# A fused attention and MoE kernel: another order of loads, units and banks at the start, weights loaded in pieces, another split of the last tile, longer half-chunks in two chunks

## The chip, the cores and the metric

The kernel runs on one core of one Trainium2 chip. The metric is device time in microseconds (us). Kernels are compared only within the same rounds. All timed runs that are compared are "fast" (none more than 1.5% above the fastest of its kernel).

## The reference, cut to what matters

```python
def _attn_ref(q, k, v):                       # (8 batches, 8 heads, 576 tokens, 64)
    scores = scale * q @ k.T                  # per batch and head
    mask = (rel >= 0) & (rel < 128)           # a sliding window of 128 tokens
    scores = where(mask, scores + slope[h] * -abs(rel), -1e9)
    return softmax(scores) @ v

def _moe_ref(x, w_in, w_out):                 # x: 4608 x 512, w_in: 512 x 2048
    h = x @ w_in                              # "MoE1"
    g = h * cos(h)
    return g @ w_out                          # "MoE2"
```

The attention's output is laid out as 4608 tokens of 512 columns and goes through the two matrix products. Inputs and output are float32; inside, the matmuls work on bf16.

## The kernel before

A small planner in the program (class `Plan`) takes the operations with guessed durations, dependencies and priorities, and fixes one order of instructions for every engine. The order cannot change at run time, and each engine runs its own in order. Where the planner expects PE to wait in the head, it puts in "fillers", matmuls of zeros.

The tokens go through MoE in 9 chunks of 512, the attention in 8 batches of 576. A chunk is MoE1 (matmul, then cosine on ScalarE and a product on VectorE) and MoE2 (matmul, copy, store). While chunk c is in MoE2, the attention of batch c+1 is woven in. A batch has 9 "units": four pairs of heads for tokens 0 to 255 ("first token group"), four for tokens 256 to 511, and a tail. ScalarE needs one table for exp (attention) and one for the cosine (MoE1); the page counts 15 table loads of 1.28 us each. An attention unit is scores, exp, mask, product with v, division, and turning the result (`xnat`) so that MoE1 can read it (`xT`):

```python
def x_back(b, u, s, i):
    ...
    pr, G = u                                   # G: token group
    t0 = S * b + 256 * G
    if b >= 3 or (b == 2 and G):                # later batches: by a transposing DMA
        o = op("sp", [lambda e: e.dma_start_transpose(
            xT[:, pr, t0:t0 + 256].rearrange("p (r t) -> p r t", r=2), xnat[i][:, :])], ...)
        xops.append(o)
        return
    ...                                         # early ones: TensorE turns, a copy follows
```

MoE1 of a chunk begins with "half" jobs, which read only 256 of its 512 tokens, so that it can start while the rest of `xT` is on its way. With SPLIT = 4 the first 8 of 16 column blocks are done in halves, first all of the first half, then all of the second, and the other 8 whole:

```python
n = (0, 8, SPLIT, SPLIT, SPLIT, SPLIT, SPLIT, SPLIT, 0)[c]
for i in range(2 * n):
    moe1_half(c, i // n, i % n, 2 + i % 6)
for i in range(16 - 2 * n):
    moe1(c, 2 * n + i, 2 + (2 * n + i) % 6)
```

Loads go through GpSimd (POOL) and convert float32 to bf16 on the way. The first ones are the head of the program; a batch's loads wait for the transposing DMAs of an earlier batch:

```python
load_first("q", q, 0, 0, "sp")      # heads 0-3, first token group
load_first("k", k, 0, 1, "sp")
...
load_half("q", q, 1)                # heads 4-7, first token group
load_half("k", k, 1)
load_v(0, (0, 1))
masks()
load_piece("q", q, 0, 1)            # second token group, 256 KB in bf16
load_piece("k", k, 0, 1)
load_w_in(0)                        # 512 of 2048 columns
load_v(0, (2, 3))
load_w_in(1)
load_w_in(2)
...                                 # tails, w_in, w_out and batch 1 mixed
# in the loop over chunks c:
if c == 0:
    load_batch(2)
elif c + 3 < B:
    load_batch(c + 3, xops[-1:])    # so batch 4 waits for batch 2's tail to land in xT
```

The last of the 36 tiles of the output is computed with 512 columns, then copied and stored in two halves:

```python
halves = 2 if tg == 4 * NCH - 1 else 1
wd = 512 // halves
for hf in range(halves):
    cs = slice(wd * hf, wd * hf + wd)
    flex(ob[oi][:, cs], ps[:, bank, cs], ...)                 # copy on ScalarE or VectorE
    op("sp", [lambda e, cs=cs: e.dma_start(out[row:row + 128, cs], ob[oi][:, cs])], ...)
```

The softmax here doesn't subtract the row's maximum and nothing guards it: scores larger than these inputs give would overflow.

## Time and profile before

| | before |
|---|---|
| time, median of 3 first runs (range) | 316.63 us (316.44 to 316.78) |
| profiled run: time, span | 317.92 us, 315.9 us |
| TensorE (PE) busy | 307.1 us, 97% |
| useful matmuls at the price of their shape | about 286 us |
| before the first matmul / after the last | 1.2 us / 3.2 us |

The profiled run was itself 1.3 us over the median.

From the profile's page of the kernel before: the span, busy time by engine, the busy tenths of PE and DMA in 40 slices of the span, and the chain that ended last by engine and by line (L843 is MoE2, L832 MoE1 in halves, L817 MoE1 whole, L611 scores).

```profile
span 315.9 us, 6775 instructions
...
PE 307.1 (97%) x2702; PEld 180.1 (57%) x2702; DVE 195.9 (62%) x440; ACT 208.2 (66%) x307; POOL 100.6 (32%) x127
...
PE   7989999999998999999999999999999999999995
...
DMA  9999999999979995599969999997813200101121
...
PE 88%; DMA 5%; ACT 3%; DVE 3%; issue 1%; POOL 0%; POOLq 0%; ACTq 0%
PE ps L843 37%; PE ps L832 20%; PE ps L817 17%; PE ps L611 5%; DMA xT<-xnat 4%; ACT p L648 2%; PE ps L705 2%; PE ps L708 1%; PE ps L526 1%; DMA qnat<-in_q_dram 1%; DVE xnat L747 1%; PE ps L780 1%; PE ps L396 1%; PE ps L691 1%; PE ps L601 1%
```

PE carries 88% of the chain, and DMA is the only other entry over 3%. PE's busy time hides stalls, because a matmul's record is longer than the distance to the next one. So I priced each matmul with the spacing of starts in a dense stretch (216 ns for 512 columns, 109 ns for 256, 29 ns for 65, 56 ns for 128) and call what exceeds that price a stall. The DMA row shows that the DMA engines are full through the first 11 slices, about 87 us.

The head, in the timeline of ScalarE (start, us, engine, line, operation, output and input, count, and in brackets the idle time before it with what ended it). The first two lines are the four exps of the first token group, the third the four of the second one, then the change to the cosine's table, then the first cosines.

```profile
7.73 1.51 ACT L648 ACTIVATE p<-ps 128x768 bf16<-128x768 f32 x2 [0.16 <-PE ps L611]
10.44 1.51 ACT L648 ACTIVATE p<-ps 128x768 bf16<-128x768 f32 x2 [1.20 <-PE ps L611]
...
15.86 3.77 ACT L648 ACTIVATE p<-ps 128x1024 bf16<-128x1024 f32 x4 [0.23 <-PE ps L611]
19.65 1.28 ACT L471 ACT_TABLE_LOAD   x1
...
21.05 1.25 ACT L803 ACTIVATE cos<-ps,halfpi 128x512 f32<-128x512 f32 x2
```

Two waits for `xT` on PE. In the first pair of lines it waits before chunk 2's second half; in the second pair, within chunk 3's first half (timeline of PE, kernel before).

```profile
92.55 1.91 PE L832 MATMUL ps<-xT,w_inb 128*128 128x256 bf16 x16
95.58 0.72 PE L832 MATMUL ps<-xT,w_inb 128*128 128x256 bf16 x5 [1.13 <-DMA xT<-xnat]
...
121.21 0.38 PE L832 MATMUL ps<-xT,w_inb 128*128 128x256 bf16 x2
121.95 0.28 PE L832 MATMUL ps<-xT,w_inb 128*128 128x256 bf16 x1 [0.36 <-DMA xT<-xnat]
```

The bracket counts from the modelled end of the last matmul, so 1.13 is 1.3 us in spacing of starts, and 0.36 is 0.5. The sum of both stands in the view of waits (who waited for whom: us in total, times, longest):

```profile
PE ps L832 <- DMA xT<-xnat: 1.5, 2, 1.1
```

The chain of the kernel before, as a list in order of time, gives the DMA that the second wait was for: from issue to landing it took over 7 us.

```profile
114.56 7.35 DMA xT<-xnat
```

The end (timeline of all engines, kernel before): the last matmuls, the stores' issues, and two copies of 256 columns that ScalarE makes one behind the other.

```profile
307.79 4.91 PE L843 MATMUL ps<-w_outb,gT 128*128 128x512 bf16 x22
...
310.02 4.05 SPq L858 DMA_DIRECT2D out_dram<-ob  x3
312.80 0.80 ACT L401 ACTIVATE ob<-ps 128x256 f32<-128x256 f32 x2 [2.86 <-PE ps L843]
```

### The profile page before, as it was taken

The page shows a single profiled execution, that of the slowest core. Times are in us where ns is not written, and L with a number is a line of the kernel's source. Part 1 is how long each engine was busy: PE and PEld are TensorE (multiplying, and loading weights), DVE is VectorE, ACT ScalarE, POOL GpSimd, SP SyncE. Part 2 cuts the span into 40 slices and gives each one's busy share as a digit, 9 for nine tenths or more (in the row PEclk, how much of TensorE's full clock was granted, in tenths as well). Part 3 has the DMA queues.
Part 4 walks back from the last instruction along what each step waited for, and adds up shares of the span by engine and source line. Part 5 has one row for each costly group of instructions (what it writes and reads, how often), then busy time and mean ns, then how long its engine had stood idle before and what let it go on. Part 6 is the DMA issues. An engine that isn't in the chain of part 4 may idle for free.

```text
span 315.9 us, 6775 instructions
## 1 busy us (share of the span) xinstructions
PE 307.1 (97%) x2702; PEld 180.1 (57%) x2702; DVE 195.9 (62%) x440; ACT 208.2 (66%) x307; POOL 100.6 (32%) x127
## 2 busy tenths in 40 slices
PE   7989999999998999999999999999999999999995
PEld 4468645685565456645764575458545844444442
DVE  3887576687666766767687578658865880353000
ACT  7788776788586857783887488739866883462211
POOL 8997650008706900491029206900000000000000
PEclk9999999999999999999999999999999999999999
DMA  9999999999979995599969999997813200101121
GB/s 124 175 197 200 192 165 193 165 138 80 183 98 111 156 174 138 93 137 172 152 99 154 191 122 133 172 183 96 150 50 87 50 0 35 67 0 68 66 97 69
DMA packets 157582, 38.97 MB, mean 123 GB/s; under 512 B 147696, under 2 KB 153072, under 8 KB 157552
## 3 DMA queue, kind: packets, MB, share of 16 engines
q0 software_dynamic: 107392, 18.10, 75.6%
q1 hardware_dynamic: 50160, 20.46, 34.1%
q8 instruction: 21, 0.34, 0.5%
q14 instruction: 9, 0.07, 0.1%
HBM read 36.70 MB, written 9.44 MB: 146 GB/s over the span
## 4 chain that ended last, share of the span: by engine, by line
PE 88%; DMA 5%; ACT 3%; DVE 3%; issue 1%; POOL 0%; POOLq 0%; ACTq 0%
PE ps L843 37%; PE ps L832 20%; PE ps L817 17%; PE ps L611 5%; DMA xT<-xnat 4%; ACT p L648 2%; PE ps L705 2%; PE ps L708 1%; PE ps L526 1%; DMA qnat<-in_q_dram 1%; DVE xnat L747 1%; PE ps L780 1%; PE ps L396 1%; PE ps L691 1%; PE ps L601 1%
## 5 line engine op out<-in xcount | busy, mean ns | idle before, releaser
L843 PE MATMUL ps<-w_outb,gT 128*128 128x512 bf16 x576 | 139.4, 379 | 0.0
L809 DVE TENSOR_TENSOR gT<-ps,cos 128x512 bf16<-128x512 f32 x144 | 94.7, 685 | 33.5 <-ACT cos L803 16.6
L803 ACT ACTIVATE cos<-ps,halfpi 128x512 f32<-128x512 f32 x144 | 94.7, 686 | 25.3 <-PE ps L832 8.3
L843 PEld LDWEIGHTS ps<-w_outb,gT 128*128 128x128 bf16 x576 | 51.5, 98 | 51.9 <-issue 0.9
L832 PE MATMUL ps<-xT,w_inb 128*128 128x256 bf16 x640 | 77.0, 273 | 2.3 <-DMA xT<-xnat 1.5
L648 ACT ACTIVATE p<-ps 128x768 bf16<-128x768 f32 (+1 forms) x64 | 54.5, 917 | 24.9 <-PE ps L611 13.0
L832 PEld LDWEIGHTS ps<-xT,w_inb 128*128 128x128 bf16 x640 | 59.9, 98 | 13.1 <-DMA xT<-xnat 2.0
L435 POOL DMA_DIRECT2D qnat<-in_q_dram x32 | 28.4, 888 | 96.5 <-DMA xT<-xtail 69.7
L817 PE MATMUL ps<-xT,w_inb 128*128 128x512 bf16 x256 | 56.7, 379 | 0.0
L401 ACT ACTIVATE ob<-ps 128x512 f32<-128x512 f32 (+1 forms) x24 | 13.9, 581 | 44.5 <-PE ps L843 44.4
L817 PEld LDWEIGHTS ps<-xT,w_inb 128*128 128x128 bf16 x256 | 25.0, 98 | 28.8 <-DVE gT L809 0.5
L444 POOL DMA_DIRECT2D vp<-in_v_dram x40 | 34.9, 939 | 5.7 <-issue 5.6
L666 DVE TENSOR_TENSOR p<-p,emask 128x1024 bf16<-128x1024 bf16 x32 | 22.0, 687 | 18.8 <-ACT p L648 18.8
L435 POOL DMA_DIRECT2D knat<-in_k_dram x32 | 28.6, 894 | 0.6 <-issue 0.6
L747 DVE TENSOR_TENSOR xnat<-ps,rec 128x256 bf16<-128x256 f32 x64 | 26.8, 421 | 2.0
L705 PEld LDWEIGHTS ps<-vp,p 128*128 128x128 bf16 x256 | 17.1, 97 | 14.4 <-issue 9.4
L705 PE MATMUL ps<-vp,p 128*128 128x65 bf16 x256 | 22.0, 193 | 0.4 <-DVE p L673 0.3
L708 PE MATMUL ps<-vp,p 128*128 128x65 bf16 x192 | 20.0, 193 | 0.0
L671 DVE TENSOR_TENSOR p<-p,emask 128x256 bf16<-128x256 bf16 x32 | 9.0, 282 | 17.4 <-ACT p L648 17.1
L471 ACT ACT_TABLE_LOAD x15 | 19.2, 1283 | 0.3
L611 PEld LDWEIGHTS ps<-qt,kt 64*128 64x128 bf16 x320 | 12.3, 95 | 11.6 <-issue 8.0
L611 PE MATMUL ps<-qt,kt 64*128 64x128 bf16 (+1 forms) x320 | 17.6, 244 | 0.5 <-DVE xT L402 0.4
(58 smaller groups left out, 169.5 us busy)
## 6 DMA issues: line engine op xcount, KB each, us to landing
out_dram<-ob SPq DMA_DIRECT2D x35, 256.0 KB, 4.1
vp<-in_v_dram POOLq DMA_DIRECT2D x32, 128.0 KB, 10.3
qnat<-in_q_dram POOLq DMA_DIRECT2D x25, 128.0 KB, 7.6
knat<-in_k_dram POOLq DMA_DIRECT2D x25, 128.0 KB, 7.9
w_inb<-in_moe_w_in_dram POOLq DMA_DIRECT2D x4, 512.0 KB, 10.8
w_outb<-in_moe_w_out_dram POOLq DMA_DIRECT2D x4, 512.0 KB, 18.0
qnat<-in_q_dram POOLq DMA_DIRECT2D x3, 256.0 KB, 17.1
knat<-in_k_dram POOLq DMA_DIRECT2D x3, 256.0 KB, 17.6
```

Of the source, the lines that this page charges most:

```text
L435: op("pool", [lambda e: e.dma_start(nat[w][b % 2][0:rows, t, :].rearrange("p (h d) -> p h d", h=H), src[b, :, 128 * t:128 * t + rows, :].r ...
L444: op("pool", [lambda e, t=t, rows=rows: e.dma_start(vp[b % 2][0:rows, t, :, 0:64], v[b, :, 128 * t:128 * t + rows, :].rearrange("h p d -> ...
L611: ins = e.matmul(ps[:, banks[x], c0:c1], keys_ap(i, x, pr, kc), query_ap(i, x, pr, qb, nb), start=True, stop=True)
L648: op("act", lambda e: e.activation(P[i][:, :, lo:512], src_[:, :, lo:512], ACTF.Exp, scale=0.125), w=held + [("P", i)], occ=920 if u[1] el ...
L705: ins = e.matmul(o, P[i][:, x, d0:d0 + 128], V[:, kc, h, 0:65], start=True, stop=not two)
L708: ins = e.matmul(o, P[i][:, x, p0:p0 + 128], V[:, kc - 1, h, 0:65], start=False, stop=True)
L747: op("dve", lambda e: e.tensor_tensor(o, U[:, :, :, 0:64], rv[:, :, :, None].broadcast_to([128, 2, 2, 64]), ALU.mult), r=[("rec", ri)], w= ...
L803: op("act", lambda e: e.activation(cosb[ci][:, :], h, ACTF.Sin, bias=halfpi[:, 0:1]), r=["halfpi"], w=[("B", bank), ("cos", ci)], occ=586, ...
L809: op("dve", lambda e: e.tensor_tensor(o, h, cs, ALU.mult), r=[("cos", ci)], w=[("B", bank)] + keys, occ=606, lat=692, pri=3)
L817: op("pe", lambda e, kc=kc: e.matmul(ps[:, bank, :], w_in[:, kc, 128 * fc:128 * fc + 128], xT[:, kc, CH * c:CH * c + CH], start=(kc == 0), ...
L832: op("pe", lambda e, i=i, fc=fc, kc=kc: e.matmul(ps[:, bank, 256 * i:256 * i + 256], w_in[:, kc, 128 * fc:128 * fc + 128], xT[:, kc, t0:t0 ...
L843: op("pe", lambda e, fc=fc: e.matmul(ps[:, bank, :], gT[gi][:, fc, 128 * t:128 * t + 128], w_out[:, fc, :], start=(fc == 0), stop=(fc == N ...
```

## The change

Its intent is to bring the start of the program closer together, so that PE is dense earlier: another order of the first loads (the later queries first, v before the weights), w_in mostly in pieces of 256 columns, another order of units and PSUM banks in batches 0 and 1. Besides, chunks 2 and 3 get 6 pairs of halves instead of 4, and the last tile is split into 384 and 128 columns, so that only a short copy and a short store follow the last matmul. The small buffers of reciprocals are separated for units and tails.

```diff
+FIRST = [("k", "q", 0, 1), ("h", "k"), ("h", "q"), ("v", 0, 0), ("v", 0, 1), ("k", "k", 0, 1),
+         ("v", 0, 2), ("v", 0, 3), ("i", 6, 2), ("i", 2, 2), ("i", 4, 2), ("i", 0, 2),
+         ("i", 12, 2), ("i", 8, 4), ("m",), ("i", 14, 2), ("k", "q", 1, 0), ("v", 0, 4),
+         ("t", "k", 0), ("o", 0, 4), ("k", "k", 1, 0), ("t", "q", 0), ("o", 4, 4), ("o", 8, 4),
+         ("v", 1, 0), ("v", 1, 1), ("o", 12, 2), ("o", 14, 2), ...]
+HEAD = [("T", "k", 0, 0, 3), ("T", "q", 0, 2, 3), ("R", (3,), (1,)), ("T", "q", 1, 7, 6), ...]
+JOBS = [(0, 6, 6), (0, 1, 1), (0, 2, 3), (1, 4, 1), (0, 4, 2), (0, 3, 5), ...]
+SECOND = [("T", "k", 0, 2, 2), ("F", 0, 6), ("T", "q", 0, 3, 3), ("R", (2,), (3,)), ...]
 ... cut: the reciprocals' buffers; keys of single 128-column blocks of w_in and w_out
-        def load_w_in(u):
+        def load_w_in(u, n=4):
 ... cut: loads n blocks of 128 columns; the same for w_out
 ... cut: the list of loads is read from FIRST, the units of batch 0 and 1 from HEAD and SECOND,
 ... the half jobs of chunk 0 from JOBS
-            halves = 2 if tg == 4 * NCH - 1 else 1
 ... cut
+                cols = [(0, 512, OB[t % 2])] if c < NCH - 1 or t < 3 else [(0, 384, 1), (384, 128, 2)]
+                for c0, wd, bank in cols:
+                    moe2_mm(c, t, bank, c0, wd)
+                    store(c, t, bank, c0, wd)
-                n = (0, 8, SPLIT, SPLIT, SPLIT, SPLIT, SPLIT, SPLIT, 0)[c]
+                n = (0, 8, 6, 6, SPLIT, SPLIT, SPLIT, SPLIT, 0)[c]
```

In FIRST, "k" is a 256 KB piece of q or k, "h" a half load of heads 4 to 7, "v" a block of v, "i" and "o" blocks of w_in and w_out, "t" a tail, "m" the masks.

## The prediction

> **What bounds the kernel.** TensorE. The page shows PE busy 307.1 of 315.9 us, clock full. Busy hides stalls, so I took the spacing of matmul starts in the timeline: a 512-column matmul costs 216 ns, a 256-column one 109 ns, a 65-column one with its own weight load 29 ns. This agrees with the Trainium skill, "TensorE: Matmul & The Clock Gate", "Back-to-back issue gap". At these prices the useful matmuls take about 286 us; the other 30 us are: 1.2 us before the first matmul, about 12.8 us of filler and stalls in 0 to 25 us, about 7 us in 25 to 100, about 5.5 us later, 3.2 us after the last matmul.
>
> **What the change does, step by step.**
>
> 1. Head (0 to 35 us). Same work, but queries of tokens 256 to 511 load first, v blocks 0 to 3 before the weights, w_in mostly in 256-column pieces. Issues on POOL: 34 instead of 32 at about 0.9 us. In the timeline the exps of the second token group start at 15.9 us, because their keys land at 12.85; the Sin table arrives at 20.9; MoE1 is dense only from 22 to 24 us. With the queries transposed while engines idle (DVE idles 3.2 us before 8.3), I expect these exps 1 to 1.5 us earlier, Sin at about 19.5, MoE1 dense from 19 to 20.5. w_in arrives at about the old rate (512 columns per 2.6 us between landings), so its first piece lands no earlier, about 15.5. Gain 2.5 us, between 1 and 4.
> 2. Batch 1 (35 to 65 us). Stalls sum to about 4 us, perhaps 2 avoidable (0.67 at 60.9, 0.42 at 40.2). But the DMA list shows landings back to back from 10 to 47 us (w_out complete at 41.1, last batch-1 v at 47.4); a PE that comes earlier meets w_out and batch 1 nearly when it did. Gain 0.7 us.
> 3. Longer halves. Before chunk 2's second half PE stands 1.3 us at 94.2 (in the waits: MoE1 halves for the DMA-transposed x). Four more half jobs are 16 more 256-column matmuls, 1.74 us of work ahead of that need: the wait disappears. The wait at 121.3 (0.5 us, chunk 3) is for the *first* half, so longer halves do not help, and PE, earlier now, may wait there more: those transposes took 7 to 9 us to land while batch 4 loaded.  Net gain 0.9 us.
> 4. Last tile. 16x512 columns (3.45 us) become 16x384 and 16x128 (2.6 + 0.9 us, estimate from the fitted spacing): equal. After the last matmul two copies of 0.39 us ran one behind the other on ACT; now one of 128 columns and a smaller store. Gain 0.5 us.
>
> Sum: 4.6 us, all on TensorE's path.
>
> **Predicted: 312.0 us, range 309.0 to 315.0.** Faster by over 2% (below 310.3): 0.25; within 2%: 0.73; slower: 0.02.
>
> **What would show it.** Step 1: Sin table load at 18 to 19.5 us (now 19.65), stalls in 0 to 25 us about 10.5 (12.8). Step 2: stalls in 35 to 65 at about 3 us. Step 3: no stall over 0.3 us near 90; the one near 118 equal or longer. Step 4: last matmul to end 2.7 us (3.2). Matmul work itself unchanged at about 286 us.
>
> **What would make it wrong.** Better: MoE1 begins at 15 us and the whole program moves up 4 us. Worse: loads of batches 0 to 3 set the pace; then PE's lead of the head comes back as waits for transposed x at chunks 2 and 3, and only the tail's half microsecond stays.

## The result, and the profile after

The kernel after took 314.97 us (median of 4, 314.78 to 315.88) against 316.53 us (316.12 to 316.78). A ratio here is the mean time of one kernel's fast runs over the mean of the other's of the same rounds, so it is not quite the ratio of the medians. It was 0.9958 (95% interval 0.9935 to 0.9980). Two later repeats on other chips gave 0.9909 and 0.9917. The mean of the three ratios, 0.993, is 2.3 us: half of the 4.6 us that I had forecast, and the first measurement is a third of it.

From the page of the kernel after (all line numbers are 16 to 18 higher: L861 is MoE2, L850 MoE1 in halves, L835 MoE1 whole, L629 scores):

```profile
span 312.9 us, 6840 instructions
...
PE 300.8 (96%) x2712; PEld 183.6 (59%) x2748; DVE 196.3 (63%) x441; ACT 207.0 (66%) x306; POOL 103.7 (33%) x131
...
PE   7699999999999998999999999999999999999996
...
DMA  9999999999999995999599999995713100201112
...
PE 84%; DMA 6%; POOL 4%; ACT 2%; issue 1%; DVE 1%; POOLq 0%; ACTq 0%
PE ps L861 37%; PE ps L850 21%; PE ps L835 15%; PE ps L629 4%; DMA w_inb<-in_moe_w_in_dram 4%; PE ps L723 2%; DMA xT<-xnat 2%; PE ps L726 2%; ACT cos L821 1%; POOL w_inb L468 1%; POOL vp L461 1%; DVE gT L827 1%; PE ps L709 1%; PE ps L711 1%; PE ps L798 1%
```

PE's busy time has fallen by 6 us, but that is no measure of gain: some matmul records are missing in this trace (the page counts 564 matmuls of MoE2 beside 592 of its weight loads). DMA's share of the chain has not fallen: 4% of it is now a load of w_in, which PE waits for in the head.

ScalarE in the head of the kernel after:

```profile
6.54 1.51 ACT L666 ACTIVATE p<-ps 128x768 bf16<-128x768 f32 x2 [0.43 <-PE ps L629]
...
10.65 0.81 ACT L666 ACTIVATE p<-ps 128x768 bf16<-128x768 f32 x1 [0.43 <-PE ps L629]
12.54 0.81 ACT L666 ACTIVATE p<-ps 128x768 bf16<-128x768 f32 x1 [1.08 <-PE ps L629]
...
15.01 3.77 ACT L666 ACTIVATE p<-ps 128x1024 bf16<-128x1024 f32 x4
18.64 0.42 ACT L417 ACTIVATE xT<-ps 128x256 bf16<-128x256 bf16 x1
19.06 1.28 ACT L489 ACT_TABLE_LOAD   x1
...
20.73 1.26 ACT L821 ACTIVATE cos<-ps,halfpi 128x512 f32<-128x512 f32 x2
```

The first two exps start 1.2 us earlier than before, but the third and fourth, which ran as a pair at 10.44, now start at 10.65 and 12.54. Those of the second token group start 0.85 us earlier, the table 0.6 us, the first cosine 0.3 us. In before the table load follows the last exp at once; here the planner has put a copy of `xT` (18.64) between them, which will matter below. PE's waits in the first 35 us (kernel after) show loads among their causes:

```profile
PE ps L723 <- issue: 1.1, 1, 1.1
PE ps L544 <- ACT kt L417: 0.8, 1, 0.8
PE ps L850 <- DMA w_inb<-in_moe_w_in_dram: 0.7, 1, 0.7
PE ps L544 <- DMA qnat<-in_q_dram: 0.6, 1, 0.6
```

A wait named "issue" was for nothing that this view shows. The one of 1.1 us at L723 ends at 11.7 us, just as the second block of v lands (11.61 in the trace's records of DMAs).

PE at chunk 2's second half and at chunk 3's first half (timeline, kernel after):

```profile
91.23 5.95 PE L850 MATMUL ps<-xT,w_inb 128*128 128x256 bf16 x53
...
118.19 0.38 PE L850 MATMUL ps<-xT,w_inb 128*128 128x256 bf16 x2
119.40 0.28 PE L850 MATMUL ps<-xT,w_inb 128*128 128x256 bf16 x1 [0.83 <-DMA xT<-xnat]
```

The wait of 1.13 us in chunk 2 is gone: 53 half matmuls run through. The wait in chunk 3 grew from 0.36 to 0.83 us. The chain of the kernel after names the same kind of DMA, again 7 us long:

```profile
112.20 7.15 DMA xT<-xnat
```

And the end (kernel after):

```profile
304.83 5.60 PE L861 MATMUL ps<-w_outb,gT 128*128 128x512 bf16 x41
...
307.70 3.40 SPq L875 DMA_DIRECT2D out_dram<-ob  x3
309.63 0.49 ACT L417 ACTIVATE ob<-ps 128x384 f32<-128x384 f32 x1 [2.00 <-PE ps L861]
310.46 0.28 ACT L417 ACTIVATE ob<-ps 128x128 f32<-128x128 f32 x1 [0.34 <-PE ps L861]
```

One copy of 0.28 us follows the last matmul, instead of two of 0.8 us in sum.

### The profile page after: what moved, and what is told of

The parts are those of the page before. It is cut to its first block, busy times and chain, and to the rows that moved or that the text cites. A ratio compares the mean times of both kernels' runs of the same rounds, so it can differ in the third digit from the quotient of the medians.

```text
span 312.9 us, 6840 instructions
## 1 busy us (share of the span) xinstructions
PE 300.8 (96%) x2712; PEld 183.6 (59%) x2748; DVE 196.3 (63%) x441; ACT 207.0 (66%) x306; POOL 103.7 (33%) x131
## 4 chain that ended last, share of the span: by engine, by line
PE 84%; DMA 6%; POOL 4%; ACT 2%; issue 1%; DVE 1%; POOLq 0%; ACTq 0%
PE ps L861 37%; PE ps L850 21%; PE ps L835 15%; PE ps L629 4%; DMA w_inb<-in_moe_w_in_dram 4%; PE ps L723 2%; DMA xT<-xnat 2%; PE ps L726 2%; ACT cos L821 1%; POOL w_inb L468 1%; POOL vp L461 1%; DVE gT L827 1%; PE ps L709 1%; PE ps L711 1%; PE ps L798 1%
## 5 line engine op out<-in xcount | busy, mean ns | idle before, releaser
L861 PE MATMUL ps<-w_outb,gT 128*128 128x512 bf16 (+2 forms) x564 | 132.4, 373 | 2.4 <-issue 1.9
L850 PE MATMUL ps<-xT,w_inb 128*128 128x256 bf16 x704 | 83.3, 273 | 1.6 <-DMA xT<-xnat 0.8
L861 PEld LDWEIGHTS ps<-w_outb,gT 128*128 128x128 bf16 x592 | 52.5, 98 | 52.4 <-issue 1.4
L850 PEld LDWEIGHTS ps<-xT,w_inb 128*128 128x128 bf16 x704 | 66.4, 98 | 11.5 <-DMA xT<-xnat 1.1
L666 ACT ACTIVATE p<-ps 128x768 bf16<-128x768 f32 (+1 forms) x64 | 54.6, 917 | 23.2 <-PE ps L629 13.7
L835 PE MATMUL ps<-xT,w_inb 128*128 128x512 bf16 x217 | 48.3, 379 | 0.4
L417 ACT ACTIVATE ob<-ps 128x512 f32<-128x512 f32 (+2 forms) x24 | 13.9, 581 | 45.6 <-PE ps L861 45.6
L835 PEld LDWEIGHTS ps<-xT,w_inb 128*128 128x128 bf16 x224 | 21.8, 98 | 25.3 <-DVE gT L827 0.5
L723 PEld LDWEIGHTS ps<-vp,p 128*128 128x128 bf16 x256 | 17.0, 97 | 14.8 <-issue 9.8
L723 PE MATMUL ps<-vp,p 128*128 128x65 bf16 x256 | 21.8, 193 | 1.3 <-issue 1.1
L629 PEld LDWEIGHTS ps<-qt,kt 64*128 64x128 bf16 x320 | 11.9, 94 | 11.2 <-issue 7.9
L629 PE MATMUL ps<-qt,kt 64*128 64x128 bf16 (+1 forms) x320 | 17.8, 239 | 0.5 <-DVE qt L418 0.3
## 6 DMA issues: line engine op xcount, KB each, us to landing
qnat<-in_q_dram POOLq DMA_DIRECT2D x3, 256.0 KB, 13.3
```

The lines of the kernel that those rows point to most:

```text
L629: ins = e.matmul(ps[:, banks[x], c0:c1], keys_ap(i, x, pr, kc), query_ap(i, x, pr, qb, nb), start=True, stop=True)
L666: op("act", lambda e: e.activation(P[i][:, :, lo:512], src_[:, :, lo:512], ACTF.Exp, scale=0.125), w=held + [("P", i)], occ=920 if u[1] el ...
L723: ins = e.matmul(o, P[i][:, x, d0:d0 + 128], V[:, kc, h, 0:65], start=True, stop=not two)
L835: op("pe", lambda e, kc=kc: e.matmul(ps[:, bank, :], w_in[:, kc, 128 * fc:128 * fc + 128], xT[:, kc, CH * c:CH * c + CH], start=(kc == 0), ...
L850: op("pe", lambda e, i=i, fc=fc, kc=kc: e.matmul(ps[:, bank, 256 * i:256 * i + 256], w_in[:, kc, 128 * fc:128 * fc + 128], xT[:, kc, t0:t0 ...
L861: op("pe", lambda e, fc=fc: e.matmul(ps[:, bank, 0:wd], gT[gi][:, fc, 128 * t:128 * t + 128], w_out[:, fc, c0:c0 + wd], start=(fc == 0), s ...
```

## The experiments

Parts of the change are told apart in time and in the trace. As marks in the trace I use the last cosine of chunks 0, 1 and 2, the first cosine of chunk 4, and the last matmul; these cosines and this matmul are the same in before and after, but the other work that is done by then is only nearly the same (the table under "mark by mark" allows for it). "Stall" is in spacing of starts.

### The tail alone

```diff
 kernel before, with only this (shortened; the copies' bookkeeping follows it):
-                moe2_mm(c, t, range(NFC), OB[t % 2])
-                store(c, t, OB[t % 2])
+                for c0, wd, bank in [(0, 384, 1), (384, 128, 2)]:     # in the last tile
+                    moe2_mm(c, t, range(NFC), bank, c0, wd)
+                    store(c, t, bank, c0, wd)
```

> The kernel before with the last tile alone changed to 384 and 128 columns; every earlier instruction stands in the same order. My theory (the tail is worth its own half microsecond, independent of the rest): 0.5 to 0.8 us under before, and 2.4 to 2.7 us from the end of the last matmul to the end of the profile instead of 3.2. Rival (a store's fixed time hides the second copy): under 0.2 us.

316.24 us against 316.78, ratio 0.9975 (0.9953 to 0.9996), which is 0.8 us. From the end of the last matmul to the end of the profile it is 2.41 us, in before 3.24. The 128-column matmuls cost 56 ns each and the 384-column ones 162.5, so the tile's 3.5 us of matmuls did not change. The theory holds: the trace shows 0.8 us, and the interval of the time (0.1 to 1.5 us) leaves zero out, though it does not size the gain.

### The longer halves alone

```diff
 kernel before, with only this:
-                n = (0, 8, SPLIT, SPLIT, SPLIT, SPLIT, SPLIT, SPLIT, 0)[c]
+                n = (0, 8, 6, 6, SPLIT, SPLIT, SPLIT, SPLIT, 0)[c]
```

> The kernel before with 6 instead of 4 pairs of halves in chunks 2 and 3. Theory of the prediction: the stall of 1.3 us before the second half of chunk 2 is gone and about 0.9 us are won in all. Rival (a lead won at chunk 2 is waited away at the first half of chunk 3, because the transposes of x land there when the loads of a later batch have ended): the stall near 94 us is gone, the one near 121 us grows by about as much, and the time is within 0.3 us of before.

316.76 us against 316.78, ratio 0.9997 (0.9979 to 1.0014). In the trace the stall near 94 us is gone and that near 119 is 0.73 us, over the 0.53 of before. The rival's time is met, its size of the second stall only partly. The granted clock (the share of TensorE's full clock) is full in this profile until 313.7 us, after the last matmul, so its mean of 0.998 touches none of the marks. This run leads the mean of before's three profiles by 1.4 us at the last cosine of chunk 2 (1.0 us if two matmuls of MoE2 that it has put off are counted) and by 0.35 us at the last matmul: a lead that is mostly lost again, as the rival says.

### The order of loads, units and banks alone

```diff
 kernel after, with only this undone:
-                n = (0, 8, 6, 6, SPLIT, SPLIT, SPLIT, SPLIT, 0)[c]
+                n = (0, 8, SPLIT, SPLIT, SPLIT, SPLIT, SPLIT, SPLIT, 0)[c]
 and the last tile again 512 columns, copied and stored in two halves
```

> The kernel after with the old last tile and 4 pairs of halves in chunks 2 and 3: only the loads, units and banks of batches 0 and 1. Theory of the prediction (head and batch 1 win 3.2 us and keep them): 2.5 to 3.5 us under before. Rival, from the profile after (the lead at the end of chunk 0 is only 0.7 us, because the last w_in pieces land no earlier, and waits at chunks 2 and 3 take part of what batch 1 adds): 0 to 1.2 us under before.

315.66 us against 316.78, ratio 0.9959 (0.9941 to 0.9977): 1.3 us, where I had predicted 3.2. That is just over the rival's range, and far from the theory's. The order's stall at chunk 3 is 1.13 us, and 0.71 at chunk 2.

### The kernel after again, twice

> The kernel after unchanged, for the sum of the parts on one chip and a second profile: 1.2 to 1.8 us under before if the first ratio stands. If the three parts are independent, their gains add up to this; if a lead is waited away, order and longer halves together win more or less than their sum.

> The kernel after unchanged, as the base of the two runs above on their chip, and a third look at how much its head varies: 1.3 to 2.9 us under before. If a late landing of single w_in loads is chance, the end of chunk 0 lies again anywhere between 32 and 34 us in the profile, and the stall near 117 us is the longer the earlier it lies.

The first repeat took 314.05 us (before 316.78, ratio 0.9909, 0.9886 to 0.9932), the second 314.60 us (before 317.12, ratio 0.9917, 0.9892 to 0.9943). The parts' sum is 0.8 + 0.1 + 1.3 = 2.2 us; after itself won 2.9 us on the parts' chip, and 2.3 us in the mean of three chips. Each of these gains has an interval of 0.5 to 0.8 us to either side, so the times do not tell whether the parts simply add up. The last cosine of chunk 0 came at 33.76, 31.98 and 33.63 us in the three profiles of one and the same kernel. And the run that was earliest there stood longest in chunk 3 (timeline of PE, first repeat):

```profile
116.57 0.38 PE L850 MATMUL ps<-xT,w_inb 128*128 128x256 bf16 x2
118.85 0.28 PE L850 MATMUL ps<-xT,w_inb 128*128 128x256 bf16 x1 [1.89 <-DMA xT<-xnat]
```

It reached the end of chunk 2 at 101.64 us, 1.6 us before the first profile's 103.26; chunk 4's first cosine came at 152.77 against 153.32, only 0.55 us earlier. The lead was waited away.

### TensorE turns x of batch 3's first token group

If PE waits for transposing DMAs there, it should gain by doing without them. The edit is legal as it stands, since batches 0 to 2 do it so. It costs 0.45 us of matmuls.

```diff
-            if b >= 3 or (b == 2 and G):
+            if b >= 4 or (b >= 2 and G):
```

> The kernel before, with x of batch 3's first token group turned by TensorE and copied (8 more matmuls of 56 ns, 4 copies of about 0.3 us), as batches 0 to 2 do it, instead of by transposing DMAs. Theory (PE waits at chunk 3's first half for these DMAs, whatever its lead): the stall of about 0.5 us near 121 us is gone and 0.45 us of matmuls are added, so the time is within 0.4 us of before. Rival (something later sets the pace): the same for the time; this run is the base for the next one.

> The kernel after with the same edit. Theory (the lead that the new order wins at the head and in batch 1 is waited away before chunk 3's first half): the stall of 1 to 2 us near 117 us is gone, the time is 0.5 to 1.6 us under after, and the gap to the kernel before with the same edit is 3 to 4 us, near the 3.2 us predicted for the head and batch 1 plus the tail. Rival (the lead is lost elsewhere, or the wait only moves to the second half or to batch 4): within 0.3 us of after.

On before: 317.48 us against 317.12, ratio 1.0007 (0.9981 to 1.0032), nothing. On after: 313.99 us, ratio 0.9906 (0.9881 to 0.9930), with after itself at 314.60 on this chip, so 0.6 us less (0.4 us by the means, with 0.7 us to either side), and no stall over 0.15 us left between MoE1's half matmuls in chunk 3. The gap between the two kernels with this edit is 3.5 us (317.48 to 313.99), without it 2.5 us (317.12 to 314.60). So the stall goes, as the theory has it; the gain has the right sign but is not clear of noise, and the rival's "within 0.3 us" is not excluded by it.

### The loads of batch 4 held back

Why do these DMAs take 7 us? The Trainium skill, "DMA: Bandwidth & Descriptors", "Issuing engines are not separate DMA queues", says that DMAs run on the same 16 DMA engines and interleave with each other, whichever engine issued them. So loads that GpSimd issued earlier would slow SyncE's transposes.

```diff
                     for g in range(0, 9, 3):
                         run(us[g:g + 3], (1, 2, 3))
+                        if c == 2 and g == 3:
+                            load_batch(4, xops[3:4])     # after the 4th transpose of batch 3 landed
...
-            elif c + 3 < B:
+            elif c + 3 < B and c != 1:
                 load_batch(c + 3, xops[-1:])
```

> The kernel after, with the loads of batch 4 issued only once the four transposing DMAs of batch 3's first token group have landed, not once batch 2's tail has. Theory (these transposes land late because the loads of batch 4 share the DMA engines; in six traces the last of the four lands within 0.5 us of the last load): they land 2 to 4 us after their issue instead of 5 to 7, and the stall near 117 us is gone; the time falls by 0.5 to 1.6 us, unless batch 4's own transposes now come too late, which would show as a wait near 140 us. Rival (the transposes are slow of themselves): they still take 5 us or more.

> The kernel before with the loads of batch 4 held back as in the third run of the call before. It is the control for that run: theory (holding them back pays because after has a lead that is waited away at chunk 3; before has little): 0 to 0.6 us under before, so the same edit that won 1.5 us on after wins at most half of that here. Rival (the edit wins the same anywhere): 1.2 us or more under before.

> The kernel after with the loads of batch 4 held back, unchanged from the earlier run, on this chip: 3.5 to 4.3 us under before if that gain was no chance of one chip.

On after: 313.11 us against 317.12 (ratio 0.9880, 0.9854 to 0.9905), 1.5 us under after on the same chip (1.2 us by the means, with 0.8 us to either side). Repeated on another chip: 313.37 against 316.85 (ratio 0.9880, 0.9861 to 0.9899). On before, as a control: 316.94 against 316.98 (ratio 1.0002, 0.9982 to 1.0023). The same edit wins 1.5 us where there is a lead to keep, and nothing where there is none. Up to the matmuls that wait in chunk 3, PE's order is the same as in after, so the loads alone differ there. Behind them the planner has ordered anew (22 more matmuls of MoE2 stand before chunk 4's first cosine, 12 more in the control), so the 1.5 us is the worth of the stall and of that order together. The stall of chunk 3 is gone (timeline of PE, the repeat; compare the 1.89 us idle in the repeat of after):

```profile
115.10 1.47 PE L861 MATMUL ps<-w_outb,gT 128*128 128x512 bf16 x6
116.41 0.82 PE L850 MATMUL ps<-xT,w_inb 128*128 128x256 bf16 x6
...
117.31 0.82 PE L850 MATMUL ps<-xT,w_inb 128*128 128x256 bf16 x6
...
118.20 1.04 PE L850 MATMUL ps<-xT,w_inb 128*128 128x256 bf16 x8
```

The trace's records of DMAs show the mechanism (us from the start; all four transposes of batch 3's first token group are meant, the fourth lands last):

| kernel | last load of batch 4 lands | fourth transpose issued, lands | stall in chunk 3 |
|---|---|---|---|
| before | 121.73 | 117.13, 122.11 | 0.53 |
| before, second profile | 119.07 | 115.52, 119.45 | none over 0.15 |
| order alone | 120.48 | 115.09, 120.69 | 1.13 |
| after | 119.33 | 114.12, 119.57 | 0.99 |
| after, first repeat | 119.01 | 112.50, 119.19 | 2.05 |
| after, second repeat | 119.56 | 113.96, 119.78 | 1.33 |
| after, batch 4 held back | 140.69 | 112.89, 115.20 | none |
| the same, repeated | 140.73 | 112.33, 114.64 | none |

With loads in flight the fourth transpose lands within 0.4 us of the last load in these rows, whenever it was issued; without them it lands 2.3 us after its issue. The first three took 6.4 to 8.7 us in the rows with loads, 2.3 to 3.9 us in the two without; PE's wait ends with the third. (In three other traces, the third of before, later keys first, and whole pieces, it came 1.0 to 1.6 us after the last load, so the tie is not exact.) In the three runs of after, PE's arrival varies by 1.6 us, and the landing by 0.6. In the first of the held-back runs PE waited later, 0.9 us for batch 4's own keys, until 151.6 us, as the expectation allowed; the repeat shows no such wait.

### Batch 1 in the old order

```diff
-SECOND = [("T", "k", 0, 2, 2), ("F", 0, 6), ...]
+SECOND = [("F", 0, 7), ("T", "q", 0, 3, 3), ("T", "k", 0, 5, 5), ("R", (0, 1, 9), (1, 2, 3)),
+          ("R", (2, 3), (1, 2)), ("T", "q", 1, 7, 7), ("T", "k", 1, 3, 3), ("F", 1, 5),
+          ("R", (4, 5, 6), (3, 1, 2)), ("R", (7, 8), (3, 1))]
```

> The kernel after with the units and banks of batch 1 in the old order (loads and batch 0 as after). In ten traces the lead over before grows from the end of chunk 0 to the end of chunk 1 by 0.8 to 1.1 us. Theory (it is batch 1's order that wins this): that growth falls under 0.3 us, and the time is 0 to 0.8 us over after, because part of a lead is waited away at chunk 3 anyway. Rival (the loads win it): the growth stays.

315.25 us against 316.98, ratio 0.9950 (0.9932 to 0.9967). From the last cosine of chunk 0 to that of chunk 1 it took 39.19 us, in before 38.85, in the three profiles of after 37.82, 37.98 and 37.76. So the lead does not grow at all, and batch 1's order is worth at least 1.0 us up to there. The time is 0.7 us over after, comparing the two ratios to before (0.9950 and 0.993), since after did not run on this chip.

### Weights in whole pieces

```diff
-         ("i", 6, 2), ("i", 2, 2), ("i", 4, 2), ("i", 0, 2),
-         ("i", 12, 2), ("i", 8, 4), ("m",), ("i", 14, 2), ...
+         ("i", 4, 4), ("i", 0, 4),
+         ("i", 12, 4), ("i", 8, 4), ("m",), ...           # and ("o", 12, 4)
```

> The kernel after with w_in in four pieces of 512 columns and the last w_out in one, the order of columns kept as far as this allows. Theory (the pieces let MoE1 of chunk 0 do more before the Sin table: first to last cosine of chunk 0 takes 12.2 us in the runs of after without a late w_in load, 13.4 in before): it takes 13 us or more again, the lead at the end of chunk 0 falls by about 1 us, and the time is 0 to 0.8 us over after. Rival (the order of units does it): 12.2 us still, time within 0.3 us of after.

> The kernel after with w_in in four whole pieces (which did no harm) and the loads of batch 4 held back (which won 1.5 us): 3.8 to 4.6 us under before, the best of the study, if the two are independent; if whole pieces only had luck, the same as the next run.

314.01 us against 316.98, ratio 0.9906 (0.9886 to 0.9925): not slower than after. First to last cosine took 14.8 us, more than either theory said, yet the end of chunk 1 came at 69.63 us, earlier than in any of the three profiles of after (69.96 to 71.58): the planner had moved work of batch 1 ahead of chunk 0's last halves, so this span was a bad mark. (The end of chunk 1 flatters it too: 4 matmuls of MoE2, 0.9 us, are put off beyond it.) By the time, the smaller pieces are not what wins. Together with batch 4 held back it took 314.05 us against 316.85 (ratio 0.9918, 0.9901 to 0.9935), less than the 3.8 to 4.6 us expected and less than the held-back kernel with pieces (0.9880). The traces say why the two need not add: with whole pieces alone PE has no wait for `xT` in chunk 3 at all (batch 4's last load lands at 117.01 us, the fourth transpose at 118.04), so there was nothing to win; with both, PE stands 0.9 us for batch 4's keys, until 135.5 us. Why those loads land earlier is open.

### Which load sets the head

```diff
 half loads first:
-FIRST = [("k", "q", 0, 1), ("h", "k"), ("h", "q"), ...
+FIRST = [("h", "k"), ("h", "q"), ("k", "q", 0, 1), ...
 later keys first:
-         ("v", 0, 0), ("v", 0, 1), ("k", "k", 0, 1), ...
+         ("k", "k", 0, 1), ("v", 0, 0), ("v", 0, 1), ...
```

> The kernel after with the two half loads (heads 4 to 7, first token group) issued before the 256 KB load of the later queries, as in before. Theory (in after these halves land at 8.7 to 9.7 us instead of 6.5 to 7.0, so the third and fourth exp start at 10.3 to 13.5 us instead of 10.1 to 11.1, and PE, in order, stands for them; this gives back the 1 to 1.5 us that I predicted for the exps of the second token group): third and fourth exp by 11 us, Sin table load at 18 to 18.7 us in the profile, chunk 0 ends 0.5 to 1.2 us earlier than the mean of after, the time is 0.2 to 0.8 us under after. Rival (the keys of the second token group, which stay where they are, or chance set this): Sin load at 18.7 to 19.8, time within 0.3 us of after.

> The kernel after with the 256 KB load of the later keys issued before the first two v loads. In seven traces with the new head the fifth exp (first of the second token group) starts at 13.9 to 15.7 us, mean 15.0, and those keys land at 12.0 to 13.7. Theory (these keys set the exps of the second token group): keys land near 10.2, the fifth exp starts by 14 us and the Sin table load by 18.3, the time is 0.3 to 1 us under after. Rival (the third and fourth exp, late behind the half loads and PE's order, and the v loads set it): fifth exp at 14.5 or later, no gain, or a loss because x of the first group waits for v.

Half loads first: 315.59 us against 316.98, ratio 0.9970 (0.9940 to 1.0000), so 1.3 us over after's mean ratio. The third exp came at 10.0 us as the theory had it, the fourth at 11.7, and the table at 18.87, in the rival's range. Chunk 0 ended at 32.85 us, 0.3 us before the mean of after. The time is lost later: the trace has 1.25 us of stall in chunk 3 and 1.1 us in chunk 5, where again the fourth transpose (185.64 us) landed with the last load (185.65).

Later keys first: 316.65 us against 316.85, ratio 1.0002 (0.9981 to 1.0023): nothing is left of the change's gain. Not all of this shows in the head: at the end of chunk 1 the profile is 1.1 us behind the mean of after, in time the run is 2.3 us behind it. Its ScalarE timeline (third and fourth exp, those of the second group, the cosine's table):

```profile
12.77 1.51 ACT L666 ACTIVATE p<-ps 128x768 bf16<-128x768 f32 x2
...
17.22 3.77 ACT L666 ACTIVATE p<-ps 128x1024 bf16<-128x1024 f32 x4 [0.16 <-PE ps L629]
...
21.31 1.28 ACT L489 ACT_TABLE_LOAD   x1
```

The keys landed at 11.5 us, later than the 10.2 expected, but before the 12.2 to 13.7 of the three profiles of after, and still these exps began 2.2 us later than in after. The rival's times hold. Its reason, that v (now landing at 12.4 and 13.3) holds PE up, is not shown: no wait for v stands in the view of PE's waits. PE stands 0.7 us for the keys, until 11.59, because its order has them before the scores of the third and fourth exp, and then runs five fillers from 12.91 to 14.48, before the first products with v. So earlier keys do not make an earlier table. Each load that comes earlier pushes the next ones back, and PE, in a fixed order, needs them all.

### Halves of the old length in the change

```diff
 kernel after, with only this undone:
-                n = (0, 8, 6, 6, SPLIT, SPLIT, SPLIT, SPLIT, 0)[c]
+                n = (0, 8, SPLIT, SPLIT, SPLIT, SPLIT, SPLIT, SPLIT, 0)[c]
```

> The kernel after with 4 instead of 6 pairs of halves in chunks 2 and 3. It sizes the longer halves within the change; alone on before they gave nothing clear. Theory (the stall of about 0.7 to 1.3 us before chunk 2's second half comes back, and the one at chunk 3's first half shrinks by as much, so only the second half of chunk 3 counts): time 0.2 to 0.9 us over after. Rival (worth the predicted 0.9 us in chunk 2 already): 0.9 us or more over after.

314.54 us against 316.85, ratio 0.9920 (0.9899 to 0.9940), the same as after's mean of 0.993, so neither expectation is met, though the interval reaches the theory's lower end. The stall before chunk 2's second half is back (0.86 us), the one in chunk 3 is 1.05 us, in the range of after's own 0.99 to 2.05. The longer halves are worth nothing that these timings can tell, with or without the rest of the change.

### Two more looks at the kernel before

> The kernel before, unchanged, for a second profile: the first one was of a run of 317.92 us, 1.3 us over its median, so leads read against it may be too large. Theory (the extra lies in the stall before chunk 2's second half or at the end, as chance of DMA landings): a span of 314 to 315 us, with the end of chunk 0 at 33.5 to 34.5 us and of chunk 1 at 72.4 to 73.3 us as in the traces of before-like kernels, so the lead of after at chunk 1 stays near 1.8 us. Rival (the whole first profile is late): both marks over 0.7 us earlier.

> The kernel before once more, for a third profile; the same expectation as of the second.

One run each, 315.86 us (granted clock 0.998) and 317.13 us. The spans are 313.8 and 315.3 us. Chunk 0 ends at 33.11 and 33.51 us, chunk 1 at 71.96 and 72.37, where the first profile had 34.47 and 73.32. Both are over 0.7 us earlier, so the rival is right: the first profile's head was a late one. The cosine's table came at 19.65 us in it and at 18.28 and 18.68 in the others.

### Where the gain stands, mark by mark

Mean of three profiles each (us from the start), before and after unchanged:

| mark | before | after | lead | lead less work put off |
|---|---|---|---|---|
| last cosine of chunk 0 | 33.70 | 33.12 | 0.6 | 0.1 |
| last cosine of chunk 1 | 72.55 | 70.98 | 1.6 | 1.4 |
| last cosine of chunk 2 | 105.68 | 102.66 | 3.0 | 2.8 |
| first cosine of chunk 4 | 155.17 | 153.20 | 2.0 | 1.6 |
| end of the last matmul | 311.79 | 310.30 | 1.5 | 1.5 |
| span | 315.03 | 312.73 | 2.3 | 2.3 |

The last column allows for work that after does behind a mark and before does ahead of it: at chunk 0 eight small matmuls that turn q and k (29 ns each) and one of MoE2 (216 ns), at chunks 1 and 2 one of MoE2, at chunk 4 two.

With all profiles that share the old head (7) or the new one (9: those of after, the order alone, the old length of halves, batch 3 by TensorE, batch 4 held back, batch 1 in the old order), chunk 0's lead is 0.9 us (33.94 to 33.03; 0.5 less the work put off), the cosine's table comes at 19.11 us in both, and third and fourth exp come 1.5 and 1.9 us later (9.66 and 10.36 to 11.18 and 12.29).

Why the table comes no earlier stands in the same traces. In the 7 with the old head the table load starts 0.02 us after the last exp. In the 9 with the new one a copy of `xT` lies between them, and the table load starts 0.28 to 1.37 us after the last exp, 0.58 in the mean: as much as these exps had won. In four of the nine ScalarE stands there for PE, which turns that x only after its first half jobs, and in three of these PE has itself waited for the first piece of w_in. The plainest case is the run with halves of the old length (PE's first half job, then ScalarE; its exps end at 17.68 us):

```profile
16.76 0.39 PE L850 MATMUL ps<-xT,w_inb 128*128 128x256 bf16 x2 [1.35 <-DMA w_inb<-in_moe_w_in_dram]
...
18.66 0.39 ACT L417 ACTIVATE xT<-ps 128x256 bf16<-128x256 bf16 x1 [0.98 <-PE ps L798]
19.05 1.28 ACT L489 ACT_TABLE_LOAD   x1
```

## Why the prediction was wrong

The direction and the bound were right; the size was not. The forecast was 4.6 us, the first measurement 1.6, the mean of three ratios 2.3. Terms of the sum, from the table above (as the marks stand; in brackets less the work put off):

1. **The head, "Gain 2.5 us, between 1 and 4": 0.6 us [0.1] (0.9 [0.5] over 16 profiles). This is the largest mis-sized term.** I had "these exps 1 to 1.5 us earlier, Sin at about 19.5". The exps of the second token group come 0.56 us earlier in the mean of the 16 profiles (15.32 to 14.76), and the table not at all. Three errors lie beneath. First, I took the table to follow these exps. In the new order a copy of `xT` comes between, at worst held up by the first piece of w_in, and it takes 0.58 us in the mean, all that the exps had won. This is read from the traces; no run moved that copy. Second, I put no price on what the loads moved back: the half loads and v come later, and the third and fourth exp come later too. That part is shown by the mean times; that reordering does not simply win it back is shown by the two experiments on loads. Third, I read the head from one profile, which was 1.0 and 1.4 us later than the two others of the same kernel. What gain there is comes after the table: first to last cosine of chunk 0 takes 13.4 us in the three profiles of before and 13.0, 12.2 and 12.2 in those of after. In part this is work put off: besides PE's, a copy of queries on ScalarE.
2. **Batch 1, "Gain 0.7 us": 1.0 us [1.2].** The run with its old order shows the growth gone. Right in mechanism, and somewhat more than forecast.
3. **Longer halves, "Net gain 0.9 us": about nothing.** The first half of the step was right: the stall of 1.3 us before chunk 2's second half is gone, and the lead grows there by 1.4 us [1.4]. The second half was under-priced. I allowed 0.4 us for "PE, earlier now, may wait there more" in chunk 3; the lead falls by 1.0 us [1.2] between the end of chunk 2 and chunk 4, in the first repeat by more. The landing of the four transposes is tied to the last load of batch 4, not to PE's arrival: the table of landings shows it, and holding batch 4 back ends it (1.5 us on after, nothing on before). The prediction named this rival under "Worse", but gave it too little weight.
4. **The tail, "Gain 0.5 us": 0.8 us.** Right in mechanism. From the last matmul to the end it is 2.4 us, 2.7 were expected; 0.5 us of the 0.8 is the copies, the rest lies around the smaller store.
5. Another 0.5 us of the lead goes between chunk 4 and the last matmul [0.1]. This is the mark and not a loss: at chunk 4's first cosine after has done two matmuls of MoE2 (0.4 us) fewer than before.

Sum of the measured terms: 0.6 + 1.0 + 1.4 - 1.0 - 0.5 + 0.8 = 2.3 us. They add up because they are differences along one table; this is no check of their causes. The version with batch 4's loads held back, 3.8 us under before by its two ratios of 0.988, is the best kernel of the study.

The signs that I had named: stalls in 0 to 25 us about 10.5 were met in one of the three profiles of after (11.5, 10.4 and 12.1 us; 12.6 in the first of before), and those in 35 to 65 us fell to 3 or further (2.8, 2.0 and 1.9), but as sums they said little. The table at 18 to 19.5 us was met at 19.06 and meant nothing, since before reaches 18.28 to 19.65. No stall near 90 and one near 118 equal or longer: met.

## What to carry to other kernels

A lead on the busiest engine is worth only what the next thing that it waits for lets through: follow the lead to the next landing, ask what that landing is tied to, and if it is other traffic on the DMA engines, move that traffic with it. A new order of loads has a price list on both sides; name what comes later, not only what comes earlier. A mark in a trace compares two kernels only if as much work lies behind it in both: count it. And a head that is paced by DMA scatters between runs by more than a small change wins, so take several profiles before pricing it.

## What the Trainium skill lacked or had wrong

- "TensorE: Matmul & The Clock Gate", "Back-to-back issue gap", gives a sustained spacing in streams of weight load and matmul of about 81 ns at 128 columns and 131 ns at 512, and says that its formula (columns / 2.4 + about 2.5 ns) is for isolated matmuls. Here such streams, each matmul with its own weight load, keep to the formula: 56 ns at 128 columns, 109 at 256, 162.5 at 384, 216 at 512.
- "DMA: Bandwidth & Descriptors", "Issuing engines are not separate DMA queues", is right about the shared engines, but puts no number on what a small transposing DMA suffers beside bulk loads: here the fourth transpose lands 2.3 us after its issue without these loads and 3.9 to 6.7 us after it with the loads of one batch in flight (six of the traces), within 0.4 us of the last of them.
- No page gives a figure for how much single loads of a steady queue scatter. In more than half of the 20 traces one or two loads of the first 27 us land 0.9 to 1.7 us later than their size's usual step (a v block 2.03 or 2.44 us after the one before, usual 0.85; a 256-column piece of w_in 2.35 after, usual 1.33), at several places; what holds them up was not looked for. In the first profile of after this hit w_in (4.26 us for a piece of 512 columns, usual 2.6) and cost PE 0.8 us at 24.8 us.
